# Another written order for the last three head pairs and the last batch of an attention and soft-MoE kernel, with other PSUM banks and two weight loads at other times

## Chip, cores and metric

The kernel runs on one core of one Trainium2 chip. The metric is the device time of one execution in microseconds; several runs of the same kernel are made, and their median is given.

## What is computed

Block-causal attention over 8 batches of 8 heads (576 positions, head size 64, mask by blocks of 64), whose output is the input of a soft mixture of experts with 8 experts of 4 slots.

```python
def _attn_ref(q, k, v):
    ...
    scores = scale * np.matmul(q, k.transpose(0, 1, 3, 2))
    ...
    scores = np.where(mask, scores, -1000000000.0)
    scores = scores - np.max(scores, axis=-1, keepdims=True)
    attn = np.exp(scores)
    attn = attn / (np.sum(attn, axis=-1, keepdims=True) + 1e-09)
    return np.matmul(attn, v).astype(np.float32)

def _moe_ref(x, phi, w1, w2):
    ...
    logits = x @ phi
    d = logits - logits.max(0, keepdims=True)
    d = np.exp(d)
    d /= d.sum(0, keepdims=True) + 1e-09
    slot_input = d.T @ x
    ...
    for e in range(E):
        h = np.maximum(slot_input[e] @ w1[e], 0.0)
        slot_out[e] = h @ w2[e]
    ...
    c = logits - logits.max(1, keepdims=True)
    c = np.exp(c)
    c /= c.sum(1, keepdims=True) + 1e-09
    return (c @ slot_out).astype(np.float32)
```

The softmax `d` runs over all 4608 rows (it is kept as a running maximum and sum over the batches), the softmax `c` over the 32 slots of each row.

## The kernel before

**Two stages.** The first (block `c1`) walks through 32 pairs of heads, numbered 0 to 31, four to a batch. For each pair TensorE makes the scores (`qk`, L461, and `qkb`, L482), VectorE the row maxima (L495, L500), ScalarE the exponentials (`expo`, L510), GpSimd the normalisation (`norm`, L528); TensorE turns the probabilities (`tr`, L548), ScalarE and VectorE copy them out of PSUM (`copy`, L391 and L393), and TensorE multiplies by v (`pv`, L580, and `pv8`, L590). For each batch follow the slot logits (`lgs`, L608 and L615), their maxima and exponentials (`stats`, L631 to L656), transposes of x (`xnat`, L717) and of the exponentials (`natural`, L667), and the slot sums (`slots`, L737, and `slots4`, L746), added to `acc` on VectorE (L755, L760). The last batch is followed by `merge` (L683 to L704), by `formed` (L765, L767), which makes the slot inputs in PSUM, and by `copied` (L772), which copies them to `siT`.

The second stage (block `c2`) is the experts: `up` (L959, 64 matmuls of 512 columns, in 16 pieces of weights of 1 MB), Relu on ScalarE (L967), a transpose on VectorE (L971), `down` (L979), a sum over groups (L909), and the outputs (`emit`, L934, L942 and L944, stored at L947 and L950). After the second piece of `up`, TensorE does the small matmul of `zsum` (L875), whose weights are `stack4`, a tile that GpSimd copies at L870; VectorE makes the factor `zinv_all` of the Relu from it.

**The logits of a batch** are copied from PSUM to a tile `lt` (`evac_l`, key `elg`) and turned from there into `c_all` (`keep_l`, key `enl`, L661 and L662). The statistics of the last batch read the logits straight from PSUM, so that nothing in the stage needs its `lt` but `keep_l`.

**The combine softmax** (`combine`, keys `comb0` and `comb1`) of the first four batches is a chain over three engines: VectorE maximum (L310), GpSimd subtraction (L311), ScalarE Exp (L316), VectorE sum, addition and reciprocal (L317 to L319), GpSimd multiplication (L320). VectorE then turns the result into `cT` (L885).

**What sets the order.** In `c1` the order of the instructions on every engine, and that of the loads on the queue of SP, is written out: each piece of work gets a number (the batch or pair times 8.6 plus an entry of the table `TM`), and the work is emitted in the order of these numbers. The table has entries of their own for the last three pairs (29, 30, 31, with the endings x, w, y), for batch 6 (ending v) and for batch 7 (ending z). `BK` gives the PSUM banks, `EN` the engine of a copy, `FILL` where matmuls on an idle tile are put between the others. `c1` and `c2` use the same PSUM one after the other: the scores, logits and sums of `c1` all lie in one tile `ps` of the whole PSUM, and the tiles of `c2` (`hp`, `so`, `o`) take its place. The same holds for the SBUF of the right side, where `lt` lies and later `stack4`.

**Weights.** 32 pieces of 1 MB: 17 are loaded during the pairs, seven (`P0` to `P6` in `TM`) into areas of the arena that the last pairs leave free, eight into the places of pieces that `up` has used.

Of the kernel before, what the change touches and what calls it, by code (L numbers as in the profile page):

```python
# [45 lines left out]
for name, n in (  # L46
# [114 lines left out]
    65.016, "en4bu": 65.2076, "pvF": 24.4174, "paF": 25.9486, "xbF": 24.6661, "xaF": 26.0784, "slu": 73.079, "sl4u":  # L161
    72.4763, "saccu": 77.2326, "sacc4u": 72.7774, "lkx": -10.2471, "lqx": -10.417, "ksx": 1.4167, "lkw": -8.6929,
    "lqw": -11.6916, "lgsv": 70.2465, "elgv": 70.3576, "UBx": 3.7596, "rm8x": 3.9614, "rm3x": 4.6004, "rm2x":
# [7 lines left out]
    "nm51x": 16.2374, "UBw": 4.0398, "gcx": 18.1469, "egcx": 20.6286, "ogcx": 18.8398, "rm8w": 4.8599, "rm3w":  # L171
# [8 lines left out]
    "nm50w": 31.1513, "nm51w": 37.8388, "UBy": 15.2566, "gcw": 50.2747, "egcw": 52.0434, "ogcw": 52.2908, "rm8y":  # L180
# [8 lines left out]
    "nm51y": 46.0497, "gcy": 46.6026, "egcy": 49.283, "ogcy": 53.4725, "gdy": 56.4664, "egdy": 56.4788, "ogdy":  # L189
    57.8677, "g7y": 36.3496, "eg7y": 46.0185, "og7y": 47.9302, "g5y": 48.084, "eg5y": 56.318, "og5y": 50.7279,  # L190
    "pvy": 58.9265, "pay": 57.7938, "xby": 61.3379, "xay": 63.4045, "lgsz": 94.5153, "elgz": 142.3154, "statsz":
    97.2378, "stats1z": 97.3265, "stats2z": 101.5187, "enlz": 144.8707, "ndtz": 118.354, "dispz": 128.2055,
# [6 lines left out]
}  # L199
# [17 lines left out]
}  # L217
FIRST = {0: "A", 1: "B", 2: "C", 3: "D", 4: "E", 5: "F"}
FILL = {"dispz": 1, "slz": 2, "siCz": 2}
NB = B  # L220
# [17 lines left out]
    "pbC": (2,), "pbD": (3,), "pbE": (7,), "pbF": (0,), "paA": (4,), "paB": (2,), "paC": (7,), "paD": (1,), "paE":  # L238
# [4 lines left out]
    "gcw": (5, 4), "gcx": (3, 0), "gcy": (0, 2), "gdw": (4, 3), "gdx": (6, 2), "gdy": (3, 5), "pbw": (7,), "pbx":  # L243
    (1,), "pby": (2,), "paw": (5,), "pax": (7,), "pay": (1,), "lgv": (3,), "lgz": (2,), "xq0v": (5, 6), "xq0z": (6,
    7), "xq1v": (0, 1), "xq1z": (5, 3), "xn4v": (4, 7), "xn4z": (1, 4), "ndv": (7, 6), "ndz": (2, 1), "slv": (5,),
    "slz": (5,), "sl4z": (1,),
}
# [5 lines left out]
def tile_attention_softmoe(  # L253
# [81 lines left out]
    with ExitStack() as c1:  # L335
# [5 lines left out]
        def bank(k, i=0, z=""):  # L341
            n = BK.get(k + z, BK.get(k))[i]
            return ps_all[:, 512 * n:512 * n + 512]
# [35 lines left out]
        def late(m):  # L379
            return {NP * NB - 1: "y", NP * NB - 2: "w", NP * NB - 3: "x", **FIRST}.get(m, f".{m % NP}")  # L380

        def tm(m, key):
            return TM.get(key + late(m), TM.get(key))
# [13 lines left out]
        def at(t, fn, *args):  # L397
            ops.append((t, len(ops), fn, args))
# [421 lines left out]
        at(tm(0, "gc") + 0.0005, fill, bank("gc", 0, late(0))[:, 384:512], 5)  # L820
        for k, n in FILL.items():
            at(te + TM[k] + 0.0005, fill, bank("xn4", 1, "z"), n)
# [229 lines left out]
```

## Time and profile before

| | us |
|---|---|
| median of 3 runs (lowest, highest) | 342.62 (342.45, 343.23) |
| the profiled execution, its own time | 343.24 |
| span of the profiled execution, first to last instruction | 340.6 |
| TensorE busy | 329.5 (97%) |
| mean granted clock of TensorE, as a share of 2.4 GHz | 0.994 |

The span leaves out what lies before the first and behind the last instruction, here 2.64 us. Busy times are sums over the span; a matmul's end is modelled, so that a row of several matmuls can overlap the next row's start. The distance from one row's start to the next row's start is therefore the better measure of what a piece of work takes on TensorE.

### The profile page before, as it was taken

Reading aid. Unit: us, or ns where it says so; the run is one execution under the profiler, and the core shown is the slowest. Engines: PE = TensorE matmul, PEld = TensorE weight load, DVE = VectorE, ACT = ScalarE, POOL = GpSimd, SP = SyncE. Lnnn points to the kernel's source line nnn. Section 1 sums busy time; section 2 is a strip of 40 time slices with the busy share of each in tenths; the row PEclk is TensorE's granted clock in tenths of the full one; section 3 lists DMA queues with packets and bytes.
Section 4 is the critical chain, followed back from the end, with each engine's and each line's share of the span. In section 5 each row is a group of like instructions: output and inputs, shape, how many; then the busy total and the mean of one; then the engine's idle time right before and its main releaser. Section 6 shows DMA issues by size and latency. Waiting matters only on the chain.

```text
span 340.6 us, 14361 instructions
## 1 busy us (share of the span) xinstructions
PE 329.5 (97%) x5674; PEld 231.0 (68%) x5674; DVE 272.3 (80%) x821; ACT 257.1 (75%) x850; POOL 205.5 (60%) x475
## 2 busy tenths in 40 slices
PE   8899999999999999999999999999999999999991
PEld 4567767767867687668766876777667876356660
DVE  5987878899888998998889988988898767473442
ACT  3998899888988898889888988998898933222332
POOL 3888784768577857785778587768766941200000
PEclk9999999999999999999999999999999999999997
DMA  5756629536653585365436763747332199999887
GB/s 181 260 155 215 230 76 317 170 88 223 186 162 102 223 272 192 102 231 163 173 107 233 248 207 93 246 114 252 94 93 65 34 345 402 394 426 413 358 335 308
DMA packets 29938, 72.28 MB, mean 212 GB/s; under 512 B 6960, under 2 KB 15280, under 8 KB 25776
## 3 DMA queue, kind: packets, MB, share of 16 engines
q1 hardware_dynamic: 29872, 71.38, 60.4%
q8 instruction: 44, 0.72, 0.8%
q14 instruction: 22, 0.18, 0.2%
HBM read 61.93 MB, written 9.44 MB: 210 GB/s over the span
## 4 chain that ended last, share of the span: by engine, by line
PE 92%; DVE 2%; DMA 1%; POOL 1%; issue 1%; SPq 1%; DVEq 0%
PE ps L580 22%; PE ps L548 16%; PE ps L461 14%; PE ps L482 11%; PE ps L590 6%; PE so L979 5%; PE hp L959 4%; PE ps L717 3%; PE o L934 3%; PE ps L608 2%; PE ps L737 2%; DMA arena<-in_k 1%; PE ps L615 1%; PE ps L746 1%; PE s_ps L909 1%
## 5 line engine op out<-in xcount | busy, mean ns | idle before, releaser
L510 ACT ACTIVATE arena<-ps,stat 128x384 f32<-128x384 f32 (+6 forms) x288 | 152.6, 541 | 25.6 <-DVE stat L495 22.2
L528 POOL TENSOR_SCALAR arena<-arena,stat 128x512 f32<-128x512 f32 (+6 forms) x288 | 151.9, 544 | 17.0 <-DVE stat L517 13.4
L495 DVE CUSTOM_DVE_ANT_1 ps<-ps,mask 128x384 f32<-128x384 f32 (+1 forms) x128 | 77.7, 637 | 7.2 <-PE ps L461 6.3
L393 DVE COPY arena<-ps 128x384 f32<-128x384 f32 (+3 forms) x134 | 68.5, 557 | 10.2 <-PE ps L548 4.5
L580 PE MATMUL ps<-arena 128*64 128x256 f32 (+2 forms) x640 | 76.1, 384 | 0.0
L391 ACT COPY arena<-ps 128x384 f32<-128x384 f32 (+3 forms) x142 | 65.2, 494 | 11.2 <-PE ps L548 7.8
L500 DVE TENSOR_REDUCE stat<-ps 128x1 f32<-128x64 f32 (+4 forms) x160 | 58.0, 403 | 6.3 <-ACT arena L510 4.1
L580 PEld LDWEIGHTS ps<-arena 128*64 128x64 f32 x640 | 40.9, 137 | 31.7 <-issue 18.8
L548 PE MATMUL ps<-ident,arena 64*128 64x64 f32 x1600 | 61.2, 226 | 1.0 <-ACT arena L510 0.6
L461 PE MATMUL ps<-arena 64*128 64x384 f32 (+1 forms) x256 | 61.2, 567 | 0.3 <-ACT arena L510 0.3
L548 PEld LDWEIGHTS ps<-ident,arena 64*128 64x128 f32 x1600 | 56.3, 139 | 4.9 <-ACT arena L510 0.8
L510 ACT ACTIVATION_READ_ACCUMULATOR arena<-ps,stat 128x1 f32 x288 | 59.2, 205 | 0.0
L482 PEld LDWEIGHTS ps<-arena 64*64 64x64 f32 x768 | 36.3, 133 | 21.0 <-ACT arena L391 4.6
L521 POOL TENSOR_SCALAR stat<-stat 128x2 f32<-128x2 f32 (+1 forms) x96 | 18.9, 197 | 47.8 <-ACT arena L510 41.6
L482 PE MATMUL ps<-arena 64*64 64x288 f32 (+4 forms) x768 | 42.8, 340 | 0.0
L461 PEld LDWEIGHTS ps<-arena 64*128 64x128 f32 x256 | 24.1, 190 | 10.4 <-DVE arena L393 4.1
L425 POOL TENSOR_SCALAR arena<-arena 128x576 f32<-128x576 f32 x32 | 21.5, 672 | 6.4 <-DMA arena<-in_k 5.0
L590 PE MATMUL ps<-arena 128*64 128x64 f32 x640 | 24.3, 223 | 0.0
L590 PEld LDWEIGHTS ps<-arena 128*64 128x64 f32 x640 | 22.6, 138 | 0.4
L393 DVE COPY xT<-ps 128x512 f32<-128x512 f32 (+1 forms) x27 | 15.3, 581 | 9.0 <-PE ps L580 8.7
L944 DVE COPY arena<-o 128x512 f32<-128x512 f32 (+1 forms) x20 | 11.7, 633 | 13.1 <-PE o L934 13.0
L495 DVE DVE_READ_ACCUMULATOR2_ANT stat<- 128x1 f32 x128 | 18.2, 142 | 0.0
(118 smaller groups left out, 286.0 us busy)
## 6 DMA issues: line engine op xcount, KB each, us to landing
arena<-in_w SPq DMA_DIRECT2D x32, 1024.0 KB, 6.5
arena<-in_k SPq DMA_DIRECT2D x32, 288.0 KB, 3.1
arena<-in_q SPq DMA_DIRECT2D x32, 288.0 KB, 3.3
out<-arena SPq DMA_DIRECT2D x18, 512.0 KB, 4.1
arena<-in_v SPq DMA_DIRECT2D x32, 256.0 KB, 3.4
arena<-in_v SPq DMA_DIRECT2D x32, 32.0 KB, 3.5
arena<-in_phi SPq DMA_DIRECT2D x1, 64.0 KB, 4.2
```

Source lines behind the costliest of these rows:

```text
L391: nc.scalar.copy(out=out, in_=in_)
L393: nc.vector.tensor_copy(out=out, in_=in_)
L425: nc.gpsimd.tensor_scalar(out=area(f"ks{m % NQB}"), in0=area(f"ks{m % NQB}"), scalar1=SCALE, scalar2=0.0, op0=ALU.mult, op1=ALU.add)
L461: nc.tensor.matmul(scores(t + str(j), m), lhsT=q[r, lo:lo + 128], rhs=k[r, 0:NC[t]], start=True, stop=True)
L482: nc.tensor.matmul(o, lhsT=a, rhs=b, start=True, stop=True)
L495: nc.vector.tensor_tensor_reduce(out=sc, in0=sc, in1=ms, scale=-1.0, scalar=-NEG, op0=ALU.add, op1=ALU.min, accum_out=st[:, 0, u:u + 1],)
L500: nc.vector.tensor_reduce(out=st[:, 0, u:u + 1], in_=scores(x, m), axis=AX.XY if x == "8" else AX.X, op=ALU.max, negate=True)
L510: nc.scalar.activation(out=pr, in_=sc, func=AF.Exp, bias=st[:, 0, u:u + 1], accum_out=st[:, 1, u:u + 1], scale=-1.0 if x[0] in "75" else 1.0,)
L528: nc.gpsimd.tensor_scalar(out=pr, in0=pr, scalar1=st[:, 2, u:u + 1], scalar2=0.0, op0=ALU.mult, op1=ALU.add)
L548: nc.tensor.transpose(out=trbank(m, g)[i][:, 64 * n:64 * n + 64], in_=prob(m, x)[r, 128 * c:128 * c + 128], identity=ident[r, r],)
L580: nc.tensor.matmul(xps[m, 0][64 * j:64 * j + 64, lo:hi], lhsT=vs(m)[:, j, c, :], rhs=rhs, start=n == 0, stop=n == 4, skip_group_check=True,)
L590: nc.tensor.matmul(xps[m, 1][64 * j:64 * j + 64, 0:64], lhsT=vs(m)[:, j, c, :], rhs=arena[:, lo:lo + 64], start=(c == 0), stop=(c == NQ - 1),)
```

## The change

Every entry of `TM` with the endings x, w, y, v and z has another number, the copies of those pairs and batches have other engines in `EN`, and their PSUM banks are others in `BK`. One fill matmul is put behind `ndt` and no longer behind `disp`. No work is added or removed.

```diff
-    "pvy": 58.9265, "pay": 57.7938, "xby": 61.3379, "xay": 63.4045, "lgsz": 94.5153, "elgz": 142.3154, "statsz":
...
-    "mg4z": 136.4427, "mg5z": 145.0335, "mg6z": 182.1376, "siTz": 166.0336, "siCz": 177.185, "comb0z": 186.5399,
-    "comb1z": 227.5308,
...
+    43.8458, "pvy": 48.3085, "pay": 44.9157, "xby": 48.7374, "xay": 46.8697, "lgsz": 76.5681, "elgz": 200.3007,
...
+    "comb0z": 175.9856, "comb1z": 183.2467,
...
-FILL = {"dispz": 1, "slz": 2, "siCz": 2}
+FILL = {"ndtz": 1, "slz": 2, "siCz": 2}
```

The pairs 29 to 31 keep the order scores, transposes, product, but their transposes and the work of batch 6 stand otherwise between each other; in the last batch the small slot matmul of batch 6 (L746) stands behind the logits of batch 7 and no longer ahead of them, and the transposes of x come in another order. On the queue of SP one weight piece is loaded before v of the last pair and no longer behind it; the last of the seven pieces that are loaded in `c1` and the fifth change places.

ScalarE at the end of the first stage. `fin` is the factor of `merge`, `c_all` the Exp of the combine softmax, `lt_5317` and `lt_5350` are the logits tile of batch 7 in the two builds, `hr` is the first Relu of the second stage. Before:

```order
L391 COPY xn<-ps 128x8x64
L697 ACTIVATE fin<-mrun_91,nmax 128x2
L391 COPY lt_5317<-ps 128x192
L316 ACTIVATE c_all<-c_all 128x576
L967 ACTIVATE hr_5403<-hp_5377,zinv_all 128x512
```

With the change:

```order
L391 COPY xn<-ps 128x8x64
L697 ACTIVATE fin<-mrun_91,nmax 128x2
L316 ACTIVATE c_all<-c_all 128x576
L391 COPY lt_5350<-ps 128x192
L967 ACTIVATE hr_5403<-hp_5377,zinv_all 128x512
```

The copy of the last logits out of PSUM has moved behind the Exp of the combine softmax.

GpSimd at the same place; `fident` belongs to `merge`, `c_all` to the combine softmax, `stack_5373` is `stack4`. Before:

```order
L676 TENSOR_TENSOR zrun<-zrun,bm_5250 128x2
L700 TENSOR_SCALAR fident<-ident,fin 128x128
L870 COPY stack_5373<-stack 128x128
L311 TENSOR_TENSOR c_all<-c_all,mx_5347 128x576
L320 TENSOR_TENSOR c_all<-c_all,mx_5347 128x576
```

With the change:

```order
L676 TENSOR_TENSOR zrun<-zrun,bm_5231 128x2
L700 TENSOR_SCALAR fident<-ident,fin 128x128
L311 TENSOR_TENSOR c_all<-c_all,mx_5342 128x576
L320 TENSOR_TENSOR c_all<-c_all,mx_5342 128x576
L870 COPY stack_5373<-stack 128x128
```

The copy that makes `stack4` has moved behind both steps of the combine softmax.

TensorE at the start of the second stage, with the engines that a row waits for; with the change:

```order
L439 LDWEIGHTS idle
L439 MATMUL ps<-idle 64x512
L959 MATMUL hp_5377<-arena,siT 32x512 [waits DVE_49,PE_49,Activation_49]
L959 MATMUL hp_5377<-arena,siT 32x512 x7
L875 MATMUL z_ps<-zrun,stack_5373 128x1 [waits Pool_49]
L959 MATMUL hp_5377<-arena,siT 32x512 x8
```

Nothing moves here: in both builds the rows stand in this order, the first L959 waits for ScalarE and L875 for GpSimd (before, L875 waits for VectorE too).

## Rows read from the trace of the kernel before

**Rows 1.** The page: busy time of each engine, share of the span.
```profile
PE 329.5 (97%) x5674; PEld 231.0 (68%) x5674; DVE 272.3 (80%) x821; ACT 257.1 (75%) x850; POOL 205.5 (60%) x475
```

**Rows 2.** Windows: busy time by engine, then granted clock, DMA share, GB/s.
```profile
260.00:270.00 10.00, 10.00 (x214) 8.12 (x210) 7.66 (x26) 9.48 (x35) 7.88 (x20) 1.00 0.22 62
...
280.00:290.00 10.00, 9.51 (x176) 6.38 (x176) 7.22 (x22) 2.92 (x12) 1.05 (x4) 1.00 0.99 407
290.00:300.00 10.00, 10.00 (x94) 3.11 (x90) 5.18 (x12) 2.06 (x3) 2.31 (x2) 1.00 0.99 401
```

**Rows 3.** Waits of TensorE over the whole span: total, times, longest.
```profile
PE ps L691 <- DVE fident L689: 0.4, 1, 0.4
```

**Rows 4.** Timeline of TensorE, start and busy time: logits of batches, pieces of a pair.
```profile
194.36 1.08 PE L608 MATMUL ps<-xT,arena 128*32 128x128 f32 x32
...
228.62 0.65 PE L608 MATMUL ps<-arena 128*32 128x128 f32 x16
...
252.56 1.79 PE L548 MATMUL ps<-ident,arena 64*128 64x64 f32 x50
254.18 1.75 PE L461 MATMUL ps<-arena 64*128 64x512 f32 x8
...
257.11 2.38 PE L580 MATMUL ps<-arena 128*64 128x256 f32 x20
...
260.00 0.58 PE L548 MATMUL ps<-ident,arena 64*128 64x64 f32 x12
...
281.41 1.05 PE L608 MATMUL ps<-xT,arena 128*32 128x128 f32 x32
```

**Rows 5.** Timeline of all engines around the start of the second stage.
```profile
286.12 0.30 ACT L391 COPY lt<-ps 128x192 f32<-128x192 f32 x1
...
287.37 0.29 POOL L870 COPY stack<-stack 128x128 f32<-128x128 f32 x1 [0.69 <-DVE fstack L699]
...
288.96 0.62 PE L439 MATMUL ps<-idle 128*64 128x512 bf16 x2
289.07 0.29 DVE L772 COPY siT<-ps 128x128 f32<-128x128 f32 x1 [0.78 <-PE ps L767]
289.28 0.15 DVE L704 TENSOR_TENSOR zrun<-zrun,fin 128x2 f32<-128x2 f32 x1
289.34 0.75 DVE L310 TENSOR_REDUCE mx<-c_all 128x18 f32<-128x576 f32 x1
289.68 1.92 PE L959 MATMUL hp<-arena,siT 128*32 128x512 f32 x16
290.18 1.16 POOL L311 TENSOR_TENSOR c_all<-c_all,mx 128x576 f32<-128x576 f32 x1 [2.52 <-DVE mx L310]
291.37 0.68 ACT L316 ACTIVATE c_all<-c_all 128x576 f32<-128x576 f32 x1 [4.95 <-POOL c_all L311]
291.54 0.38 PE L875 MATMUL z_ps<-zrun,stack 128*128 128x1 f32 x2
291.85 4.93 PE L959 MATMUL hp<-arena,siT 128*32 128x512 f32 x44
...
293.49 1.16 POOL L320 TENSOR_TENSOR c_all<-c_all,mx 128x576 f32<-128x576 f32 x1 [2.16 <-DVE mx L319]
...
296.08 0.69 ACT L967 ACTIVATE hr<-hp,zinv_all 128x512 f32<-128x512 f32 x1 [4.03 <-DVE zinv_all L880]
```

**Rows 6.** Windows behind the last matmul, columns as in the second group.
```profile
335.00:336.00 1.00, 0.00 (x0) 0.00 (x0) 0.00 (x0) 0.00 (x0) 0.00 (x0) 1.00 1.03 422
...
337.00:338.00 1.00, 0.00 (x0) 0.00 (x0) 0.00 (x0) 0.00 (x0) 0.00 (x0) 0.50 1.03 422
```

**Rows 7.** Timeline of TensorE: the first matmuls of the span, and the last.
```profile
0.95 3.62 PE L432 MATMUL ps<-idle 128*64 128x512 bf16 x8 [0.95 <-DVE zrun L291]
...
5.89 1.32 PE L482 MATMUL ps<-arena 64*64 64x288 f32 x24
...
329.94 3.10 PE L934 MATMUL o<-cT,s 32*128 32x128 f32 x32
```

More of the change, by code (lines that the diff above doesn't have):

```diff
@@ L161 @@
     65.016, "en4bu": 65.2076, "pvF": 24.4174, "paF": 25.9486, "xbF": 24.6661, "xaF": 26.0784, "slu": 73.079, "sl4u":
-    72.4763, "saccu": 77.2326, "sacc4u": 72.7774, "lkx": -10.2471, "lqx": -10.417, "ksx": 1.4167, "lkw": -8.6929,
-    "lqw": -11.6916, "lgsv": 70.2465, "elgv": 70.3576, "UBx": 3.7596, "rm8x": 3.9614, "rm3x": 4.6004, "rm2x":
[7 rows of a table removed]
-    "nm51x": 16.2374, "UBw": 4.0398, "gcx": 18.1469, "egcx": 20.6286, "ogcx": 18.8398, "rm8w": 4.8599, "rm3w":
[8 rows of a table removed]
-    "nm50w": 31.1513, "nm51w": 37.8388, "UBy": 15.2566, "gcw": 50.2747, "egcw": 52.0434, "ogcw": 52.2908, "rm8y":
[8 rows of a table removed]
-    "nm51y": 46.0497, "gcy": 46.6026, "egcy": 49.283, "ogcy": 53.4725, "gdy": 56.4664, "egdy": 56.4788, "ogdy":
-    57.8677, "g7y": 36.3496, "eg7y": 46.0185, "og7y": 47.9302, "g5y": 48.084, "eg5y": 56.318, "og5y": 50.7279,
-    "pvy": 58.9265, "pay": 57.7938, "xby": 61.3379, "xay": 63.4045, "lgsz": 94.5153, "elgz": 142.3154, "statsz":
-    97.2378, "stats1z": 97.3265, "stats2z": 101.5187, "enlz": 144.8707, "ndtz": 118.354, "dispz": 128.2055,
[6 rows of a table removed]
+    72.4763, "saccu": 77.2326, "sacc4u": 72.7774, "lkx": -7.5111, "lqx": -11.0805, "ksx": -6.7646, "lkw": -8.5203,
+    "lqw": -5.648, "lgsv": 68.0776, "elgv": 70.9835, "UBx": 3.3957, "rm8x": 4.4399, "rm3x": 7.1427, "rm2x": 4.7319,
[7 rows of a table added]
+    14.0807, "nm51x": 16.3604, "UBw": 5.3154, "gcx": 16.1253, "egcx": 20.0534, "ogcx": 17.9671, "rm8w": 6.2568,
[8 rows of a table added]
+    17.5147, "nm50w": 27.5433, "nm51w": 22.8561, "UBy": 12.9389, "gcw": 34.6349, "egcw": 40.1565, "ogcw": 36.5463,
[8 rows of a table added]
+    33.3433, "nm51y": 28.524, "gcy": 34.2896, "egcy": 42.8294, "ogcy": 35.3528, "gdy": 43.912, "egdy": 44.7118,
+    "ogdy": 46.7181, "g7y": 24.1648, "eg7y": 32.7291, "og7y": 28.7751, "g5y": 37.3777, "eg5y": 44.3303, "og5y":
+    43.8458, "pvy": 48.3085, "pay": 44.9157, "xby": 48.7374, "xay": 46.8697, "lgsz": 76.5681, "elgz": 200.3007,
+    "statsz": 77.9425, "stats1z": 80.8463, "stats2z": 87.0098, "enlz": 297.6852, "ndtz": 108.0906, "dispz":
[6 rows of a table added]
 }
@@ L238 @@
     "pbC": (2,), "pbD": (3,), "pbE": (7,), "pbF": (0,), "paA": (4,), "paB": (2,), "paC": (7,), "paD": (1,), "paE":
[4 rows of a table removed]
[L243 to L246, printed above, removed]
[4 rows of a table added]
+    "gcw": (2, 3), "gcx": (4, 1), "gcy": (1, 3), "gdw": (4, 1), "gdx": (2, 5), "gdy": (4, 0), "pbw": (5,), "pbx":
+    (7,), "pby": (6,), "paw": (4,), "pax": (2,), "pay": (1,), "lgv": (7,), "lgz": (3,), "xq0v": (4, 2), "xq0z": (5,
+    2), "xq1v": (0, 5), "xq1z": (7, 1), "xn4v": (4, 0), "xn4z": (4, 6), "ndv": (1, 6), "ndz": (7, 1), "slv": (1,),
+    "slz": (4,), "sl4v": (2,), "sl4z": (2,),
 }
```

75 rows, old and new, of tables (BK, EN, TM) are left out of this document.

## The prediction

> **What bounds the kernel now.** I read the page's first part, then the windows over the end of the span, then the waits of TensorE, then the timeline. TensorE is busy for 329.5 of 340.6 us [rows 1]. In the windows the reader is to see that it stays so where the change is made: 10.00 of 10 us from 260 to 270, 9.51 from 280 to 290, 10.00 from 290 to 300 [rows 2]. The one wait of TensorE for data around the last batch is 0.4 us, for VectorE at L691 [rows 3]. So the time is the sum of what TensorE does plus the little that it stands still. The same matmuls are there with the change; it can win only what stands still now, and it loses whatever new stillness it makes. The timeline shows where the first stage hands over to the second: the slot inputs are copied at 289.07 (L772), two fill matmuls run from 288.96 to 289.58, and the first L959 starts at 289.68 [rows 5].
>
> **The change, part by part.**
>
> *The handover, first wait.* The first L959 waits for ScalarE, because its PSUM was part of `ps` and ScalarE's last read of `ps` is the copy of the last logits to `lt`. Before, that copy ran at 286.12 and was over 3 us ahead of L959 [rows 5]; it cost nothing. With the change it stands behind the Exp at L316 on ScalarE, and L316 waits for GpSimd (L311), which waits for VectorE (L310), which comes behind the copy at L772. So the first L959 now waits for a chain that starts only when the slot inputs are already there. Its rungs are in [rows 5]: L310 starts at 289.34 and ends at 290.09, L311 runs from 290.18 to 291.34, L316 from 291.37 to 292.05. Behind it the copy of `lt` takes 0.30. The hops between these rows are 0.03 and 0.09 us; with 0.03 and 0.05 for the last two, the copy ends at 292.38 and L959 starts at 292.43. From this goes 0.06, the distance from the start of L704 at 289.28 to that of L310, since L704 no longer stands between L772 and L310. That is 292.37 in place of 289.68: +2.7 us. The lower end is 2.55, if ScalarE starts the copy a little ahead of the Exp's end; the upper is 2.8. Queued behind L959 is all the work of TensorE.
>
> *The handover, second wait.* After two pieces of L959 (1.86 us, from 289.68 to 291.54 [rows 5]) TensorE comes to L875, which needs `stack4`. Before, GpSimd copied it at 287.37, early [rows 5]. Now it stands behind L320, which starts at 293.49 and takes 1.16: its end is 294.65, less the same 0.06, and with hops of 0.02 and 0.05 around the copy's 0.29 us, L875 can start at 294.95. TensorE would be there at 292.37 + 1.86 = 294.23. So it waits another 0.7, and L875 stands 3.4 us behind its old 291.54. The second wait thus takes up the error of the first: if the first is only 2.55, the second is 0.85. Nothing is late behind it: the Relu at 296.08 waited 4.03 us for `zinv_all` [rows 5], which VectorE makes behind L885 and L875. L885 follows L320 as before, L875 now ends at 294.95 + 0.38 = 295.33, so `zinv_all` comes at about its old time, while the sums that the Relu reads will be complete only at 291.85 + 3.4 + two pieces at 0.87 = 297.0. The Relu then waits for TensorE instead, which costs TensorE nothing.
>
> *The last three pairs.* A pair takes 1.62 us of transposes (252.56 to 254.18), 2.93 of scores (to 257.11) and 2.89 of products (to 260.00), 7.44 together [rows 4]. A batch takes 34.26 (logits at 194.36 to logits at 228.62), so its own work is 34.26 - 4 x 7.44 = 4.50. From 260.00 to the last logits at 281.41 stand three sets of transposes, one of scores, three of products and one batch's work: 4.86 + 2.93 + 8.67 + 4.50 = 20.96 of 21.41 us. So the old order loses 0.45 there, and no other order can win more. It can lose more: in the new one the three sets of transposes of pair 29 come at once behind the products of pair 28, where the old one spread them over 6 us, and VectorE, ScalarE and GpSimd are busy 7.66, 9.48 and 7.88 of 10 us there [rows 2]. No row prices this; two waits of the one size seen, 0.4 [rows 3], make 0.8. Between -0.45 and +0.8 I take 0, as the old order's loss is nearest to a typical one. In the last batch the slot matmul of batch 6, now behind the logits, fills TensorE's time while VectorE works on the statistics, but VectorE takes over the copies of `dn` and does L704 ahead of the sums: between -0.4, the wait at L691 gone, and +0.4, I take 0. The copies that change engines and the PSUM banks are part of these two bounds. The moved fill is the same matmul at another place: 0.
>
> *The weights.* One piece is issued ahead of the scores of pair 31, in the stretch where the DMA engines are 0.22 busy [rows 2]. A gain is excluded: TensorE has no wait for weights among its waits. A loss would need v of the last pair, now queued behind this 1 MB, to come late; it is issued behind the products of pair 29, and used behind those of pair 30 and two sets of transposes, 2.89 + 2 x 1.62 = 6.1 us later [rows 4]. The two pieces that change places are first needed in `down`, far later. 0 for both.
>
> *The sum.* 2.7 + 0.7 + 0 + 0 = +3.4 us. From 291.85 on TensorE runs on as before, and behind the last matmul (329.94 + 3.10 = 333.04 [rows 7]) the last outputs drain in 7.6 us, all of it shifted. The profiled execution of 343.24 (span 340.6, 2.64 around it) would become 346.6. Its 343.24 is 0.62 above the median of the runs, so the median goes from 342.62 to 346.0.
>
> **A rule against it: the clock.** TensorE would stand still from 289.58 to 292.37, 2.8 us. In the trace the granted clock is still 1.00 at 335 to 336, two to three us behind the last matmul at 333.04, and 0.50 at 337 to 338 [rows 6]. So stillness does drop it from 2.4 to 1.2 GHz there, but not at once. The Trainium skill, "TensorE: Matmul & The Clock Gate", section "HAM oscillation — how this bites in real kernels", says that a wait between two bursts of matmuls can throttle TensorE again, so that the next burst starts cold. By that rule the start of `up` would run at the lower clock; no stretch of this trace has such a gap with work behind it. What it would cost is in the rows: at the start of the span eight matmuls of 512 columns on the idle tile take 3.62 us, 0.45 each, against 0.31 for each of the two at 288.96, and by 5.89 a row of scores takes 1.32 us as it does later. So the low clock held for some 4.7 us of work (0.95 to about 5.7) [rows 5, 7], half of which is lost: 2.4.
>
> **Rivals.**
> (a) *The clock falls* in the new gap: 3.4 + 2.4 = +5.8, 348.4. For it speaks that it falls at the end of the span; against it that it was still up at 335 to 336. 0.08.
> (b) *Only the first wait counts*, because GpSimd's copy is placed or released earlier than its row in the order says: +2.7 at most, 2.55 at least, 345.2. Against it stands its place behind L320. 0.08.
> (c) *The new order of the pairs loses too*: +3.4 + 0.8 = 346.8 or, with the last batch, 347.2. 0.12. The opposite, a win of 0.85 in both, gives 345.2. 0.07.
> (d) *Not slower.* The order names for L959 a wait on ScalarE, not for which of its instructions. If it were one ahead of L316, such as L697 at its old time, the first wait is nothing; if the same holds for L875, the second too, and the pairs' and the batch's bound decides: -0.85 to +0.8, 341.8 at best. It decides from a `lt` copy that is done by 289.6. Against it: the copy reads `ps`, which `hp` replaces, and that read must be over. 0.03, of which 0.02 faster by over 0.2%.
>
> **How the numbers follow.** The likeliest case, both waits and nothing else, has 0.62 and 346.0, from 345.5 to 346.5. The range of 344.9 to 347.5 takes in (b) and (c) with both signs, and leaves out (a) and (d), 0.11, and a little for what I do not see. What a measurement of this kernel can tell from no change is about 0.2%, 0.7 us; every case but (d) is slower by more: slower 0.96, same 0.02, faster 0.02.
>
> **What would show it.** Right: a gap of 2.7 us on TensorE ahead of the first L959, with ScalarE's copy of `lt` (L391) as its releaser; a second of 0.7 ahead of L875, released by GpSimd's L870; ScalarE's L316 ahead of the copy; the last logits within 0.8 us of 281.4, and the same distance from there to L772; no granted clock below 1.00 before the last matmul. Wrong: L959 within 0.3 us of the end of the fills, (d); no gap at L875, (b); rows of L959 longer than 0.87 us a piece, (a); waits of TensorE on transposes of pairs 29 to 31 that sum to over 1 us, (c).

## The result, and the profile after

The changed kernel takes 346.53 us, median of 6 runs (345.97 to 348.68), the kernel before 343.15 beside it, median of 6. The ratio is 1.0113, 95% interval 1.008 to 1.0145; it goes by the means, 346.83 and 342.96, and leaves out one run of the kernel before that took 1736.19 us. The changed kernel is slower, by 3.4 us by these medians and 3.9 by the means. The profiled execution took 345.97 us, its span 344.2 (before 343.24 and 340.6): the span grew by 3.6, and what lies outside it is 1.8 here where it was 2.64.

TensorE's busy time is nearly the old one [rows 1], so the time went where it stands still or runs slowly:

```profile
PE 330.5 (96%) x5674; PEld 230.6 (67%) x5674; DVE 271.9 (79%) x820; ACT 257.5 (75%) x851; POOL 206.6 (60%) x475
```

The windows of the changed kernel (busy time by engine, granted clock, DMA share, GB/s) show the place, in steps of one us and at the end over 10 us as in [rows 2]:

```profile
290.00:291.00 1.00, 0.00 (x0) 0.00 (x0) 0.00 (x0) 0.00 (x0) 1.00 (x1) 1.00 1.00 418
291.00:292.00 1.00, 0.00 (x0) 0.00 (x0) 0.12 (x1) 0.83 (x2) 0.13 (x1) 0.69 0.27 98
292.00:293.00 1.00, 0.89 (x8) 0.24 (x12) 0.93 (x3) 0.06 (x1) 0.00 (x0) 0.50 0.06 25
293.00:294.00 1.00, 1.00 (x12) 0.34 (x8) 0.52 (x3) 0.00 (x0) 0.71 (x1) 0.50 0.00 0
294.00:295.00 1.00, 1.00 (x12) 0.01 (x2) 0.52 (x1) 0.00 (x0) 0.68 (x2) 0.60 0.00 0
295.00:296.00 1.00, 1.00 (x10) 0.46 (x10) 0.54 (x3) 0.00 (x0) 0.00 (x0) 1.00 0.80 156
...
290.00:300.00 10.00, 7.89 (x62) 2.32 (x66) 3.61 (x10) 1.58 (x3) 2.53 (x3) 0.83 0.60 211
```

Where TensorE was busy for 10.00 of 10 us from 290 to 300, it is now busy for 7.89, and the mean granted clock there is 0.83: from inside 291 to 292 until inside 294 to 295 the lower of the two levels, 1.2 GHz, holds. The waits of TensorE have a new first line, and the one for L691 [rows 3] is gone:

```profile
PE hp L959 <- ACT lt L391: 2.7, 1, 2.7
...
PE ps L746 <- DVE dn L393: 0.5, 1, 0.5
```

The timeline of all engines at the handover answers to [rows 5]:

```profile
288.83 0.62 PE L439 MATMUL ps<-idle 128*64 128x512 bf16 x2
288.94 0.29 DVE L772 COPY siT<-ps 128x128 f32<-128x128 f32 x1 [0.91 <-PE ps L767]
289.15 0.74 DVE L310 TENSOR_REDUCE mx<-c_all 128x18 f32<-128x576 f32 x1
289.98 1.16 POOL L311 TENSOR_TENSOR c_all<-c_all,mx 128x576 f32<-128x576 f32 x1 [3.56 <-DVE mx L310]
291.17 0.68 ACT L316 ACTIVATE c_all<-c_all 128x576 f32<-128x576 f32 x1 [5.23 <-POOL c_all L311]
291.76 0.30 ACT L391 COPY lt<-ps 128x192 f32<-128x192 f32 x1
...
292.11 3.23 PE L959 MATMUL hp<-arena,siT 128*32 128x512 f32 x16 [2.65 <-ACT lt L391]
...
293.29 1.16 POOL L320 TENSOR_TENSOR c_all<-c_all,mx 128x576 f32<-128x576 f32 x1 [2.16 <-DVE mx L319]
...
294.39 0.29 POOL L870 COPY stack<-stack 128x128 f32<-128x128 f32 x1
...
295.26 0.38 PE L875 MATMUL z_ps<-zrun,stack 128*128 128x1 f32 x2
295.58 3.21 PE L959 MATMUL hp<-arena,siT 128*32 128x512 f32 x28
```

The first L959 has stood still for 2.65 us, waits for the copy of the last logits (`lt`), and starts at 292.11 instead of 289.68. Its first two pieces take 3.15 us (292.11 to 295.26) where they took 1.86, because they run at half clock. L875 comes without a wait: the stack it reads was ready at 294.68. L959 resumes at 295.58 in place of 291.85, 3.73 later, and the last L934 starts 3.58 later [rows 7]:

```profile
333.52 3.10 PE L934 MATMUL o<-cT,s 32*128 32x128 f32 x32
```

**How the runs are compared.** Ahead of the handover the same kernel differs by up to a microsecond from execution to execution (in three profiles of the changed kernel L772 starts at 288.94, 288.71 and 289.13, and in the experiments built from it at 288.87 to 289.91; a stall of 0.5 to 1 us in one of the earlier batches of some profiles, and the start of the span, make it). So the experiments are read by a stretch inside each profile: from the start of L772, where the slot inputs are ready, to the start of the last L934. It is 289.07 to 329.94, 40.87 us, in the kernel before, of which there is one profile, and 288.94 to 333.52, 44.58, in the changed one.

### The profile page after: what moved, and what is told of

It is laid out like the page before. It is cut to its first block, busy times and chain, and to the rows that moved or that the text cites. A ratio compares the mean times of both kernels' runs of the same rounds, so it can differ in the third digit from the quotient of the medians.

```text
span 344.2 us, 14368 instructions
## 1 busy us (share of the span) xinstructions
PE 330.5 (96%) x5674; PEld 230.6 (67%) x5674; DVE 271.9 (79%) x820; ACT 257.5 (75%) x851; POOL 206.6 (60%) x475
## 4 chain that ended last, share of the span: by engine, by line
PE 91%; DVE 2%; POOL 1%; DMA 1%; issue 1%; ACT 1%; SPq 1%; DVEq 0%; ACTq 0%
PE ps L580 21%; PE ps L548 16%; PE ps L461 14%; PE ps L482 11%; PE ps L590 6%; PE hp L959 4%; PE so L979 4%; PE o L934 3%; PE ps L717 3%; PE ps L608 2%; PE ps L737 2%; DMA arena<-in_k 1%; PE ps L615 1%; PE ps L746 1%; PE ps L667 1%
## 5 line engine op out<-in xcount | busy, mean ns | idle before, releaser
L391 ACT COPY arena<-ps 128x384 f32<-128x384 f32 (+3 forms) x142 | 65.2, 493 | 10.7 <-PE ps L548 7.7
L548 PE MATMUL ps<-ident,arena 64*128 64x64 f32 x1600 | 60.5, 226 | 1.0 <-ACT arena L510 0.6
L461 PEld LDWEIGHTS ps<-arena 64*128 64x128 f32 x256 | 23.9, 188 | 10.7 <-DVE arena L393 4.1
L959 PE MATMUL hp<-arena,siT 128*32 128x512 f32 x128 | 15.4, 638 | 2.7 <-ACT lt L391 2.7
```

Of the source, the lines that this page charges most:

```text
L391: nc.scalar.copy(out=out, in_=in_)
L461: nc.tensor.matmul(scores(t + str(j), m), lhsT=q[r, lo:lo + 128], rhs=k[r, 0:NC[t]], start=True, stop=True)
L548: nc.tensor.transpose(out=trbank(m, g)[i][:, 64 * n:64 * n + 64], in_=prob(m, x)[r, 128 * c:128 * c + 128], identity=ident[r, r],)
L959: nc.tensor.matmul(hps[nh][NS * g:NS * (g + 1), :], lhsT=siT[:, c, :], rhs=pieces[i][:, g, :], start=(c == 0), stop=(c == 3), tile_positio ...
```

## Experiments

The table has every profile, counted from the start of L772; the ends of the half clock, in the time of each profile's span, are worked out from the granted clock in windows of 1 us.

| kernel | first L959 | L875 | last L934 | half clock, us of the span |
|---|---|---|---|---|
| before | +0.61 | +2.47 | +40.87 | none |
| both waits undone, two profiles | +0.62, +0.61 | +2.47, +2.47 | +40.73, +40.72 | none |
| changed, three profiles | +3.17 each | +6.32, +6.51, +6.74 | +44.58, +45.33, +46.13 | 291.4 to 294.8, 291.5 to 294.9, 291.5 to 298.3 |
| before, with late `lt` and stack only | +3.24 | +6.34 | +45.09 | 293.3 to 296.7 |
| changed, fills | +3.17 | +5.80 | +44.07 | none |
| changed, early stack | +3.17 | +6.74 | +45.97 | 291.6 to 298.5 |
| changed, fills and early stack, two profiles | +3.17, +3.17 | +5.02, +5.02 | +43.35, +43.63 | none |
| changed, `lt` early, stack late | +0.61 | +5.80 | +45.74 | 295.5 to 299.0 |

### Both waits undone

The diffs of `TM` here and below show the changed entries alone, out of longer lines of the table.

```diff
-"elgz": 200.3007,
+"elgz": 142.3154,
...
-"enlz": 297.6852,
+"enlz": 144.8707,
```

> The changed kernel with the copy of lt and the numerators of the last pair put back to their old places ahead of the queue (both waits undone; the new order of the last pairs, the other PSUM banks and the moved weights stay). Theory (the whole loss is the handover into the last batch's output): the 2.7 us wait of L959 goes, L959 begins near 289.6 instead of 292.1, L875 has its operand when PE comes to it, the granted clock stays 1.00 from 289 to 296, and the time is that of the kernel before to within 0.3%, by the traces 0.1 to 0.2 us below it, as the first copy of siT ended 0.13 earlier. Rival (the new order of the pairs or the moved weights lose by themselves): 0.8 us or more above the kernel before, with the loss ahead of 289 or behind 297.

343.13 us, median of 12 runs, against 342.98 of the kernel before: a ratio of 1.0009, interval 0.999 to 1.0028. The timeline of TensorE at the handover and its end:

```profile
289.80 0.62 PE L439 MATMUL ps<-idle 128*64 128x512 bf16 x2
290.53 1.92 PE L959 MATMUL hp<-arena,siT 128*32 128x512 f32 x16
292.38 0.38 PE L875 MATMUL z_ps<-zrun,stack 128*128 128x1 f32 x2
...
330.64 3.10 PE L934 MATMUL o<-cT,s 32*128 32x128 f32 x32
```

L959 follows the fills with no wait named, and L875 its first two pieces after 1.85 us. Two numbers are put back, and the whole loss is gone, though the new order of the pairs, the banks and the weights are all still there. The rival falls. No gain is left either: the time is that of the kernel before to within the interval, and none of the versions tried here beats it. The second number, `enlz`, belongs to the transposes that read `lt` (L661, L662). `stack4` takes the place of `lt`, and GpSimd's copy to it names the second of them as its releaser here:

```profile
288.18 0.33 POOL L870 COPY stack<-stack 128x128 f32<-128x128 f32 x1 [0.92 <-DVE c_all L662]
```

So the late transposes are what made the copy of the stack late; the kernel with the second wait alone, below, differs from this one in `enlz` only.

### The two late copies alone, in the kernel before

```diff
-"elgz": 142.3154,
+"elgz": 230.3007,
...
-"enlz": 144.8707,
+"enlz": 297.6852,
```

> The kernel before with two entries of the order alone taken from the change: the copy of lt behind the Exp of L316, and the last numerators late; the old order of the pairs, the old banks and the old weights stay. Theory: all of the loss comes with these two, 3.3 to 3.8 us over the kernel before, the same wait of L959 for ScalarE (2.4 to 2.8 us), the same stretch of half clock inside it and in the 3 us behind it. Rival (the loss needs the new order of the pairs too): under 2.5 us.

347.26 against 342.98, a ratio of 1.0126, interval 1.0093 to 1.0159. The wait, and windows (columns as above):

```profile
PE hp L959 <- ACT lt L391: 2.7, 1, 2.7
```

```profile
293.00:294.00 1.00, 1.00 (x9) 0.14 (x5) 0.92 (x5) 0.00 (x0) 0.05 (x1) 0.65 0.12 49
...
296.00:297.00 1.00, 1.00 (x10) 0.58 (x14) 0.43 (x3) 0.00 (x0) 0.00 (x0) 0.64 0.82 344
```

The same wait appears with the old order of the pairs, so these two entries are enough for the loss. The expected 3.3 to 3.8 us was too low: it is 4.22 by the stretch and 4.3 by the medians, as the half clock lies later here. It begins at 293.3, when L959 is already running (292.77), and reaches past L875 (295.87).

### Fills in the gap

```diff
-FILL = {"ndtz": 1, "slz": 2, "siCz": 2}
+FILL = {"ndtz": 1, "slz": 2, "siCz": 12}
```

> The changed kernel with twelve idle matmuls behind the first copy of siT instead of two, so that PE is busy until about 291.4 while L959 waits. Theory (after the wait, the half clock costs what the second wait would have cost, and a little more): the clock stays 1.00, L959 still begins near 292.1, its first 16 take about 0.93 us and the next two pieces are through by 294.0, L875 then waits until about 294.75 for the stack, and the time is 0.3 to 0.6 us below the changed kernel, still 3.0 to 3.4 above the kernel before. Rival (the clock is the larger part, as 16 matmuls of 3.15 us for two pieces against 1.86 suggest when taken alone): 1.2 us or more below the changed kernel. Rival (the clock costs nothing here): the time of the changed kernel.

347.22 against 342.98, a ratio of 1.0115, interval 1.0085 to 1.0145. The timeline of TensorE:

```profile
289.60 2.78 PE L439 MATMUL ps<-idle 128*64 128x512 bf16 x12
292.88 1.92 PE L959 MATMUL hp<-arena,siT 128*32 128x512 f32 x16 [0.50 <-ACT lt L391]
295.51 0.38 PE L875 MATMUL z_ps<-zrun,stack 128*128 128x1 f32 x2 [0.70 <-POOL stack L870]
```

One of the windows, between the fills and the two pieces:

```profile
292.00:293.00 1.00, 0.50 (x6) 0.12 (x8) 0.35 (x1) 0.83 (x2) 0.00 (x0) 1.00 0.20 66
```

With TensorE at work in most of the gap the granted clock is 1.00 in every window from 288 to 304, the two pieces take 1.92, and the second wait comes out from under the half clock: 0.70 us at L875, for GpSimd's copy. The stretch is 44.07, 0.51 below the first profile of the changed kernel, as the theory had it; the rival of 1.2 us or more is met when the other two profiles of the changed kernel (below) are taken instead. The time does not show any of this; the 0.3 to 0.6 us that the theory promised there did not come. From the last L934 to the end of the span go 11.9 us here and 10.7 in the kernel before, so in this profile the end took back more than the clock gave.

### The stack early

```diff
+        at(te + TM["siCz"] + 0.001, lambda: nc.gpsimd.tensor_copy(
+            out=fident.rearrange("p (g s) -> p g s", g=4), in_=stack.unsqueeze(1).broadcast_to([128, 4, NS])
+        ))
...
-        stack4 = t2.tile([128, 4, NS], F32, name="stack4")
-        nc.gpsimd.tensor_copy(out=stack4, in_=stack.unsqueeze(1).broadcast_to([128, 4, NS]))
-        stack4 = stack4.rearrange("p g s -> p (g s)")
+        stack4 = fident
```

> The changed kernel with the copy of stack that L875 reads made early and into a place of its own, so that L875 waits for GpSimd no more; the copy of lt stays late. Theory (the second wait lies under the half clock): L959 at 292.1, half clock from 291.4 to 294.8, L875 at 295.2 to 295.3, the time of the changed kernel to within 0.3 us. Rival (the second wait is still paid, as the prediction had it): 0.5 to 0.7 us below the changed kernel.

347.51 against 342.98, a ratio of 1.0126, interval 1.0097 to 1.0155. The two added lines shift the line numbers behind them by one. The timeline of TensorE, then the windows:

```profile
292.82 3.64 PE L960 MATMUL hp<-arena,siT 128*32 128x512 f32 x16 [2.66 <-ACT lt L391]
296.39 0.59 PE L876 MATMUL z_ps<-zrun,fident 128*128 128x1 f32 x2
```

```profile
291.00:292.00 1.00, 0.00 (x0) 0.00 (x0) 0.00 (x0) 0.12 (x1) 0.84 (x1) 0.82 0.95 393
...
298.00:299.00 1.00, 1.00 (x12) 0.14 (x8) 0.00 (x0) 0.00 (x0) 0.00 (x0) 0.76 1.02 418
```

Taking the second wait away brings nothing, as expected, but the stretch of 45.97 is not that of the first profile to within 0.3 either, so the theory is missed there: the half clock lasts from 291.6 to 298.5 here, twice as long. That raised the question whether the clock's part is the same in each execution.

### Fills and early stack together

The edits of the last two in one kernel.

> The changed kernel with both edits of the two runs before this: twelve idle matmuls behind siT, and the stack copied early for L875; the copy of lt stays late. Counted from the start of L772 to the start of the last L934 (40.87 us in the kernel before, 44.58 in the changed one, 44.1 with the fills alone, 46.0 with the early stack alone). Theory (the first wait is the copy of lt and costs about 2.55; the second wait is real, but is paid only where the clock does not fall; the half clock is paid where nothing waits behind it): no half clock, no wait ahead of L875, 43.3 to 43.5 us, 0.7 below the fills alone and 2.5 below the early stack alone. Rival (fills or the place of the stack cost something by themselves): 44 or more. Rival (the clock still falls): 45 or more.

346.09 against 342.40, a ratio of 1.0104, interval 1.0075 to 1.0132. The timeline of VectorE and TensorE:

```profile
288.87 0.29 DVE L772 COPY siT<-ps 128x128 f32<-128x128 f32 x1 [0.91 <-PE ps L767]
...
292.04 1.92 PE L960 MATMUL hp<-arena,siT 128*32 128x512 f32 x16 [0.50 <-ACT lt L391]
...
293.89 0.38 PE L876 MATMUL z_ps<-zrun,fident 128*128 128x1 f32 x2
...
332.22 3.10 PE L935 MATMUL o<-cT,s 32*128 32x128 f32 x32
```

Neither half clock nor second wait: 43.35 us. That separates the parts, by one profile of each kernel. The first wait alone costs 43.35 - 40.72 = 2.63; the second, with the clock up, 44.07 - 43.35 = 0.72; the clock, with nothing behind it that waits, 45.97 - 43.35 = 2.62. By the second profile of this kernel (43.63, below) the three would be 2.91, 0.44 and 2.34; L875 itself waits 0.70 in the kernel with the fills.

### The second wait alone

```diff
-"elgz": 200.3007,
+"elgz": 142.3154,
```

> The changed kernel with the copy of lt put back ahead of the Exp, so that the first wait is undone, and the last numerators and with them GpSimd's copy of the stack left late: the second wait alone. Theory (the two waits are in a row, so the second takes up what the first does not take): L959 begins 0.6 us behind the start of L772, and after its first two pieces L875 waits for the stack until some 5.8 us behind it, a wait of about 3.3 us; with the clock at 1.00 that makes 44.1 to 44.2 us from L772 to the last L934, and nearly the whole loss of the changed kernel is there with one half of the cause. As the stillness is as long as that ahead of L959 was, the clock may fall in it too; then the work behind runs at half clock for some us with no second wait to hide it, 1.5 to 3 us more, 45.6 to 47. Rival (the second wait is worth the 0.7 that the prediction gave it): 41.6 us.

348.01 against 342.40, a ratio of 1.0144, interval 1.0098 to 1.0189. The timeline of TensorE, then the windows:

```profile
290.00 1.92 PE L959 MATMUL hp<-arena,siT 128*32 128x512 f32 x16
...
295.19 0.38 PE L875 MATMUL z_ps<-zrun,stack 128*128 128x1 f32 x2 [3.26 <-POOL stack L870]
```

```profile
294.00:295.00 1.00, 0.00 (x0) 0.00 (x0) 0.07 (x1) 0.00 (x0) 1.00 (x2) 1.00 1.04 410
295.00:296.00 1.00, 0.81 (x6) 0.50 (x10) 0.93 (x4) 0.00 (x0) 0.13 (x1) 0.77 1.01 418
296.00:297.00 1.00, 1.00 (x8) 0.20 (x4) 0.23 (x1) 0.00 (x0) 0.00 (x0) 0.50 1.00 426
```

With the first wait undone L875 waits 3.26 us, where the theory had 3.3 and the rival 0.7: the two waits stand in a row on one chain, and whichever comes last takes up what the other leaves. So half of the repair is no repair. The clock falls here too, only behind the gap, so all of its price is paid: 45.74, within the 45.6 to 47 foreseen for that case. Three of the four runs took 347.62 to 348.53 and one 345.72. This one has a mean granted clock of 0.996 over its span of 343.8 us, which leaves some 2.8 us at the half level in all, less than the shortest stretch of the table (3.4); so in that run the clock can hardly have fallen here.

### The changed kernel again, twice

> The changed kernel itself once more, beside the two others. Theory (in the gap ahead of L959 the clock falls at a point that differs from run to run, so its price does): the first wait of 2.65 us again, 44.0 to 46.0 us from L772 to the last L934, depending on how far the half clock reaches. Rival (the first profile is what each run does): 44.6 to within 0.1, with the clock falling 1.9 us behind the last fill.

> The changed kernel a third time. Theory (the first wait is fixed, the clock's fall is not): L959 waits 2.65 us for ScalarE's copy of lt, the half clock begins 1 to 4 us behind the last fill, and 44.1 to 46.0 us go from L772 to the last L934. Rival (the half clock always begins in the gap and ends with the second piece of L959): 44.6 to 45.3.

347.00 against 342.40 in the first (ratio 1.0121, interval 1.0079 to 1.0162), 348.24 against 343.28 in the second, a single run. The wait of L959 is 2.65 us in both. The timeline of TensorE in the first:

```profile
291.88 3.41 PE L959 MATMUL hp<-arena,siT 128*32 128x512 f32 x16 [2.65 <-ACT lt L391]
...
315.77 0.43 PE L979 MATMUL so<-arena,hT 128*32 128x128 f32 x8 [0.57 <-issue]
```

and the windows of the second:

```profile
291.00:292.00 1.00, 0.00 (x0) 0.00 (x0) 0.00 (x0) 0.64 (x2) 0.32 (x1) 0.75 0.50 197
...
297.00:298.00 1.00, 1.00 (x8) 0.19 (x4) 0.11 (x1) 0.00 (x0) 0.00 (x0) 0.50 1.05 442
298.00:299.00 1.00, 1.00 (x12) 0.31 (x8) 0.00 (x0) 0.00 (x0) 0.00 (x0) 0.84 1.00 303
```

The rivals, that each execution is like the first, fall; so does the theory's upper end, by 0.13. One and the same kernel has 44.58, 45.33 and 46.13, that is 0.51, 1.26 and 2.06 above the kernel with fills (44.07). A fourth case is among the six runs of the result: one has a mean granted clock of 0.996 over its span of 344.2 us, again some 2.8 us at the half level in all, so the clock can hardly have fallen in its gap; it took 346.00. In the second profile 0.57 of the 1.26 is probably not the clock: TensorE waits at 315.77 for nothing that the waits name. A weight piece landed at 315.61, right ahead of it, so it is likely a weight that comes late because the loads into the places of `up` start only when L959 has used them, first issued at 293.87 here and at 290.80 in the kernel before. That was not tried by itself.

### The two repaired kernels again

> The kernel with the fills and the early stack once more. In its first profile the stretch from L772 to the last L934 was 43.35 us, as foreseen, but from there to the end of the span went 11.9 us in place of 10.7: over the last 1.2 us one sixteenth of the DMA rate was left. Theory (one DMA engine lags behind the other fifteen, in some executions of any of these kernels): the first stretch 43.3 to 43.4 again, the end 10.7 or up to 2 longer, independent of it. Rival (with the clock up, TensorE delivers the outputs too fast for the DMA engines, so the loss is only moved to the end): 11.9 again, with all sixteen busy to the end.

> The kernel with both waits undone once more. In its first profile the stretch from L772 to the last L934 was 40.73 us and the end 12.6. Theory (a lagging DMA engine, by chance): 40.7 to 40.9 again, and the end is 10.7 or up to 2 longer. Rival (the moved weight pieces leave one engine behind each time): 12.6 again.

Single runs: 347.18 and 342.51 against 343.28. With both waits undone the stretch is 40.72 and the end 10.7 us, so the 12.6 of its first profile does not belong to this order. With fills and early stack the stretch is 43.63, 0.2 above the range (0.18 of it is a wait of TensorE at L980 that names no releaser), and the end 11.9 again. The windows of that end:

```profile
342.00:343.00 1.00, 0.00 (x0) 0.00 (x0) 0.00 (x0) 0.00 (x0) 0.00 (x0) 0.50 0.55 221
343.00:344.00 1.00, 0.00 (x0) 0.00 (x0) 0.00 (x0) 0.00 (x0) 0.00 (x0) 0.50 0.05 20
```

In the last of them the DMA engines are 0.05 busy, less than one of sixteen, so one works on alone, and the rival (all sixteen busy to the end) falls. All three profiles of the two kernels with twelve fills have this end, and of the other nine one in full (12.6) and one in part (11.2); the other seven have 10.7.

The traces show what goes with it. In these five, and in none of the seven, one transfer of the instruction queue (`q8 instruction` of the DMA view, 16 KB, 1.0 to 1.3 us) runs while the last outputs are being stored: from 334.95 to 336.22 in this profile. In the seven it comes only after the outputs, as at 342.44 in the kernel before, where the span ends at 340.6. So the end goes with the time at which that transfer is made, and the kernel with both waits undone has it in one profile and not in the other. That the transfer is what keeps the one engine back is not shown, as the views do not tell the engines apart, and why all three profiles with fills have it is open.

By the times the gain shows less than by the stretches. The kernel with both edits has 346.09 against 347.00 of the changed kernel beside it, 0.9 lower where the stretches of the two profiles differ by 1.98, and the fills alone (347.22) are not lower at all; the longer end is the likely reason.

## Why the prediction was right, and which terms were off

**The time.** Forecast 346.0, measured 346.53, inside 344.9 to 347.5 and just above the likeliest case's own range (345.5 to 346.5). The direction and the place were right: undoing the two waits undoes the loss (1.0009), and the two alone make it (1.0126). That the number came so near is partly luck. Several terms were off and made up for each other, as the next paragraphs show, and in the second set of runs the changed kernel is 4.6 us above the kernel before (347.00 and 342.40), not 3.4.

**First wait, +2.7.** Right in mechanism and releaser, a little large: L959 comes 3.17 behind L772's start in place of 0.61, which is 2.56, and the cost by experiment is 2.63. The copy of `lt` began at 291.76, 0.09 ahead of the Exp's end, the overlap that set the lower bound of 2.55.

**Second wait, +0.7.** It exists, and with the clock up it costs 0.72. In the changed kernel as it is, TensorE does not show it, since the half clock makes the two pieces ahead of it 1.29 us longer and the copy is ready by then. The prediction's sign for that, a gap of 0.7 at L875, was absent, which it had named as the sign of rival (b); but the reason is not that rival's: GpSimd's copy stands behind L320, where the order put it.

**The last three pairs and the last batch, 0.** The sum is right, the two terms are not. From the logits of batch 5 to L772 go 60.45 us before (228.62 [rows 4] to 289.07) and 60.57 in the changed kernel (228.37 to 288.94), 60.49 in the second profile of the kernel with both waits undone (228.85 to 289.34). But the sign that the prediction gave, the last logits within 0.8 us of 281.4 and the same distance from there to L772, was not met. The timeline of TensorE in the changed kernel:

```profile
228.37 0.65 PE L608 MATMUL ps<-arena 128*32 128x128 f32 x16
...
280.46 1.06 PE L608 MATMUL ps<-xT,arena 128*32 128x128 f32 x32
```

and in the kernel before, ahead of its last logits:

```profile
281.19 0.40 PE L746 MATMUL ps<-xn,dn 128*32 128x128 f32 x8
```

From logits to logits go 52.09 us in place of 52.79, and from the last logits to L772 8.48 in place of 7.66. The slot matmul that changed sides (L746) takes 0.22 of this (281.19 to 281.41 [rows 4]). The difference is not chance: it is 52.1 in every profile with the new order and 52.8 in both with the old one. Without L746 the pairs became about 0.5 shorter, all that the prediction thought an order could win there (0.45), and the last batch about 0.6 longer, beyond its bound of 0.4. TensorE's wait of 0.4 at L691 was exchanged for one of 0.5 at L746; where the rest of the 0.6 lies was not looked into. The two cancel, which is luck. A loss in the pairs, rival (c), is excluded.

**The weights, 0.** Nothing waits for the two moved pieces. What the prediction did not see is that the other pieces come later because of the gap, as TensorE frees their places later; in one profile of three this may have cost 0.57, which is argued and not tried.

**The clock: the step that failed.** The prediction said that no granted clock below 1.00 would show ahead of the last matmul, and gave rival (a), +2.4 for the clock, 0.08. It reasoned from the end of the span, where the clock was still up two to three microseconds behind the last matmul [rows 6]. In the changed kernel it fell inside the gap, at 291.4, only 1.9 us behind the last fill (over at 289.45). The two pieces then took 3.15 us, 1.6 each, over the 0.87 that the prediction had named as the sign of rival (a). The sum came out nevertheless, because in that execution the half clock took the place of the second wait and added only 0.51 to it; the other two profiles lie 1.26 (0.57 of it the wait at L979) and 2.06 above the kernel with fills. So the terms are 2.6 + 0.7 and 0.5 to 2.1 for the clock, and by the stretch the three profiles lose 3.7, 4.5 and 5.3 to the kernel before: the prediction's 3.4 is a little below all of them. With 2.62 in the kernel with the early stack, rival (a)'s price of 2.4 was about right for a half clock of nearly 7 us with nothing behind it; that it and the second wait overlap was the part that the rival had not worked out, adding 3.4 and 2.4. The rival drew its price from the lengths of matmuls alone: the windows of the kernel before read 1.00 from 1 to 6 us too, where its trace has no clock record ahead of 5.64, and 0.31 for a fill at full clock is too long, as twelve of them take 2.78, 0.23 each. The rule of the Trainium skill, "TensorE: Matmul & The Clock Gate", section "HAM oscillation — how this bites in real kernels", that a wait between two bursts can throttle TensorE again, holds here: the first 16 matmuls behind the gap took 3.15 us against 1.86.

## What to carry to other kernels

A copy out of PSUM belongs to the critical path of whatever takes the place of its tile next, even if nobody reads the copy soon: before moving it behind a chain on its engine, look for who writes there next. Here the tile `ps` spans all of PSUM, so the first matmul of the next stage waited for the last reader of any part of it; whether a tile of its own for the logits would have avoided the wait was not tried. Two late operands on one chain are one loss, not two: putting back the first alone left the full loss (3.26 us at L875 in place of 2.65 at L959), and only both together removed it. A gap on TensorE like the 2.65 us here should be priced with the slower clock behind it, by a range (0.5 to 2.6 us in these kernels) and not by a number, and one profile of it is too few.

## What was not expected of the hardware

Where the half clock begins and how long it lasts differs between executions of the same kernel with the same gap of 2.65 us: from 291.4 to 294.8, from 291.5 to 294.9 and from 291.5 to 298.3. With a gap of 3.26 us, in the kernel with the late stack alone, the granted clock was 1.00 to the end of the gap and fell only in the window from 295 to 296, after TensorE had taken up its work at 295.19; so the fall can come when the engine is busy again. With ten more idle matmuls, which fill most of the gap, it was 1.00 in all three profiles that had them. And the end of the span was 0.5 to 1.9 us longer in five of twelve profiles, with one DMA engine's worth of work or less at its very end (windows of 0.04 to 0.06 busy, of sixteen engines); each time a transfer of the instruction queue had run among the last outputs, and in the other seven profiles it had not.
